# A threshold attention followed by a routed attention: the threshold as a parametric ReLU on ScalarE, transposed weights copied by VectorE, and the last queries of two pairs in 64x64 quarters of TensorE

## The chip, the cores and the metric

One core of one Trainium2 chip runs the whole program. The metric is device time in microseconds (us); lower is better. The kernel before took 880.97 us, the median of three runs (880.44 to 881.66). A run is told from no change here when it differs by more than about 0.2%, some 1.8 us.

## The reference, cut to what matters

Two attentions stand behind each other. The first has 8 batches of 8 heads, 576 queries and keys, 64 features. Every score that lies more than `tau` below the largest of its row is dropped before the softmax:

```python
scores = scale * np.matmul(q, k.transpose(0, 1, 3, 2))
thresh = np.max(scores, axis=-1, keepdims=True) - tau
scores = np.where(scores >= thresh, scores, -1000000000.0)
scores = scores - np.max(scores, axis=-1, keepdims=True)
attn = np.exp(scores)
attn = attn / (np.sum(attn, axis=-1, keepdims=True) + 1e-09)
return np.matmul(attn, v).astype(np.float32)
```

The heads are put side by side (512 features), and the second attention, called MoE below, projects them for four experts of 64 features, does a causal softmax attention for each, multiplies by an output matrix and adds the two experts that a gate picks for each row. The change does not touch its arithmetic.

## The kernel before, in words

Work goes by **pairs** of heads: 32 pairs (8 batches of 4), and the two heads of a pair lie in partitions 0 to 63 and 64 to 127. After the four pairs of a batch comes the MoE part of that batch (`moe`).

For pair n, `prep` loads k, q and v, transposes k and q on TensorE and lets ScalarE copy them to `kx` and `qx`. The 576 queries are cut into four **main tiles** of 128 (s = 0 to 3) and a **tail** of 64 (s = R = 4).

- `scores` (line 821). A main tile makes two score blocks of 128 queries by 576 keys, one for each head, in four matmuls of 64 rows by 128 columns of the array, so that both heads use one half each. The tail makes one block: head 0's 64 queries in partitions 0 to 63, head 1's in 64 to 127, by four matmuls on 128 rows and 64 columns, with the zero padded tiles `tk` and `tq`. For each block of 128x576, VectorE copies PSUM to `sc` and takes the row minimum (`copied_min`, line 661; q is scaled by -1/8, so it is minus the maximum), GpSimd adds tau to it (`thr`, line 628, one column), ScalarE takes `exp` (line 672), VectorE compares with `thr`, multiplies and sums the row (`stt`, line 650), VectorE inverts the sum (lines 627 and 639), and GpSimd multiplies the row by it (line 628) into `pp`.
- `transp` and `transp_tails` transpose `pp` in 128x64 pieces on TensorE (line 1161), and `blocks_out` lets ScalarE copy the two PSUM banks into `pt`, `pt4` and `ptt` (line 600).
- `attnv` multiplies by v (64 columns of the array for each head) and splits the result into a high and a low part `x`.

Nothing is run in the order in which the code names it. A `Plan` records every operation with a key, which is its pair's number plus an offset from the table `PLACE` (by step) and one from `PLACE_OP` (by engine and tile). `arrange` plays them on five engines with fixed costs and writes down the order, and each engine then runs its own list strictly in that order. Where the planner foresees TensorE idle in the first 80 us, `fill` puts in matmuls on a constant tile `still` (line 1158), whose result nobody reads. Buffers come from small families (`SLOTS`: 5 of `pp`, 3 of `sc`, 5 of `pt`). All eight PSUM banks are shared: scores take two neighbouring banks a block (family `s`), all else one (family `g`).

Of the kernel before, what the change touches and what calls it, by code (L numbers as in the profile page):

```python
# [22 lines left out]
SLOTS = {"ki": 2, "qi": 2, "qx": 2, "kx": 2, "pp": 5, "st": 2, "vm": 2, "p2": 3, "sc": 3, "pt": 5, "pt4": 2,  # L23
         "ptt": 2, "x": 12, "v2": 1, "q2": 2, "zt": 2, "z0": 2, "z1": 2, "pt2": 4}
PLACE = {
# [19 lines left out]
    "av1": 1.4444, "kT": -1.0327, "later": 1.7433, "load": -1.3911, "perm": 3.2453, "qT": -0.7341, "qload": -1.2168,  # L45
# [4 lines left out]
}  # L50
PLACE_OP = {
    "ACT gw": 0.1842, "ACT kx": -0.5027, "ACT lg": 1.2177, "ACT p2": 1.9457, "ACT pp": -1.6841, "ACT pt": -2.7791,
    "ACT pt2": 1.5279, "ACT pt4": 0.1304, "ACT ptt": -3.9332, "ACT q2": -3.6685, "ACT q2d0": -2.4746,
    "ACT q2d1": -1.3511, "ACT qi": -2.1752, "ACT qx": 1.2312, "ACT tau_t": 1.1034, "ACT tq0": -1.9086,
    "ACT v2": 4.4888, "ACT warm": 1.5459, "ACT wkh": 2.3421, "ACT woh": -1.794, "ACT wqh": -1.3238, "ACT wvh": 3.8984,
    "ACT x": -4.5167, "ACT z0": 3.8315, "ACT z1": 1.547, "ACT zt": 2.9762, "DVE col": 0.2892, "DVE gate": -3.09,
    "DVE gt": 1.9765, "DVE gw": 5.359, "DVE lg": 1.016, "DVE p2": 3.9028, "DVE pp": -0.5531, "DVE q2": 6.2857,
    "DVE qsc": -2.8622, "DVE sc": -0.1035, "DVE st": -1.4447, "DVE still": -0.4814, "DVE tau_p": 0.8807,
    "DVE v2": 2.0003, "DVE warm": 0.2939, "DVE x": 0.3195, "DVE z0": 2.2304, "DVE z1": 0.159, "DVE zt": 2.0055,
    "PE g": -1.5017, "PE s": 1.4698, "POOL col": -3.0293, "POOL ident": 6.5183, "POOL mask": 2.2701,  # L60
    "POOL mask2": -1.5054, "POOL p2": -1.7322, "POOL pp": 1.1515, "POOL q2d0": 1.9326, "POOL q2d1": -0.4273,
    "POOL st": -4.7961, "POOL tie": -4.1632, "POOL tk0": -1.7488, "POOL tk1": -4.6506, "POOL tq0": 3.2991,
    "POOL tq1": -0.284, "POOL vtx0": 0.099, "POOL vtx1": -1.8361, "POOL vtz0": -1.5424, "POOL vtz1": -1.4797,
    "POOL wkl": 0.1504, "POOL wol": 2.3037, "POOL wql": 1.3512, "POOL wvh": -0.2325, "POOL wvl": -5.4675,
    "SP ki": 0.3554, "SP lg": 0.4166, "SP out": -1.7257, "SP qi": 1.0657, "SP st": 0.188, "SP tk0": 2.4441,
    "SP tk1": -6.0235, "SP tq0": 1.1743, "SP tq1": -1.2151, "SP vm": -1.3425, "SP vtx0": -1.0912, "SP vtx1": 1.4099,
    "SP vtz0": -1.3099, "SP vtz1": 1.2953,
}
AV_GROUPS = ((4, 0, 1), (2, 3))
AHEAD = 3  # L70
LAST_OUT = 3
CHANGE = ((0, 150, 205, 150), (205, 0, 205, 150), (205, 150, 0, 0), (205, 150, 60, 0))
EXP_SB = True
# [55 lines left out]
class Op:  # L129
    def __init__(self, e, busy, late, outs, ins, fn, at):  # L130
        self.e, self.busy, self.late, self.outs, self.ins, self.fn = e, busy, late, outs, ins, fn
        self.base, self.unit = at
        own = f"{self.unit}@{self.base:g}"
        self.unit = own if own in PLACE else self.unit
        self.kind = e + " " + (outs[0].v.fams[0] if outs else "out")
        self.key = self.base + PLACE[self.unit]
        self.mode = 0
        self.pre = set()
        self.dma = False
# [6 lines left out]
class Plan:  # L146
# [68 lines left out]
    def network(self):  # L215
# [43 lines left out]
        for v in tiles:  # L259
            if inside(v):  # L260
                g = of[v.ops[0]]
                needs[g].append(v)
                for n in v.ops:
                    if ops[n].e != "PE":
                        for r in ops[n].outs:
                            if r.v not in needs[g] and not any(ops[x].e == "PE" for x in self.writers(r.v)):
                                needs[g].append(r.v)
# [14 lines left out]
    def arrange(self):  # L282
# [11 lines left out]
        for v in sorted(tiles, key=lambda v: (turn[v], v.index)):  # L294
            if not inside(v) and v.fams[0] != "col":
# [14 lines left out]
        tiled = [0]  # L310

# [22 lines left out]
        def allot(g, t):  # L334
            got, taken, step = [], set(), defaultdict(int)
            for v in needs[g]:
                if v.slot is not None:
                    continue
                if not inside(v) and v.fams[0] != "col":
# [15 lines left out]
        while wake:  # L355
# [19 lines left out]
            for v, s in got:  # L375
# [3 lines left out]
                if not inside(v) and v.fams[0] != "col":  # L379
# [8 lines left out]
            if ops[g].dma:  # L388
                t = max(t, landed[-8])
                landed.append(t + ops[g].late)  # L390
            at[g] = t
# [95 lines left out]
def kernel(  # L487
# [48 lines left out]
    def const(name, shape, dtype=F32):  # L536
# [5 lines left out]
             "p2": 2 * SM, "sc": S, "pt": 2 * SM, "pt4": 7 * P, "ptt": 2 * P, "x": S, "v2": (R + 1) * E * D, "q2": 2 * S,  # L542
# [15 lines left out]
    def matmul(o, x, y, start, stop):  # L558
        w = size(y)
        rows, cols = x.shape[0], size(x)  # L560
        form = 2 if rows == 64 else 1 if cols == 64 else 0
# [6 lines left out]
        if form:  # L568
            t /= 2
# [4 lines left out]
    def transposed(x, y, blocks):  # L574
        for n, (a, b) in enumerate(blocks):
            for o, i, sl in ((x, a, heads[0]), (y, b, heads[1])):
                half_transpose(o[:, n * D:(n + 1) * D], i[sl], sl)
# [97 lines left out]

    def dma(dst, src, e="SP", more=0):
# [21 lines left out]
    tau_p = const("tau_p", [P, 1])  # L698
    qsc = const("qsc", [P, 1])
# [8 lines left out]
    scaled("DVE", tau_p, tau_t, 0.0, op0=ALU.max)  # L708
# [58 lines left out]

    def values_in(n):
        b, hp = divmod(n, NPAIR)
        plan.place = (n, "vload")  # L770
        vm = plan.tile("vm", [P, 2, R, D], F32)
        dma(vm, v[b, 2 * hp:2 * hp + 2, :SM, :].rearrange("h (p r) d -> p h r d", r=R))
        for j in range(2):
            dma(vtz[n % 2][heads[j], j], v[b, 2 * hp + j, SM:, :])
            dma(vtx[n % 2][heads[1 - j], j], v[b, 2 * hp + j, SM:, :])
        return vm, vtz[n % 2], vtx[n % 2]

    def prep(n):
# [3 lines left out]
        tk, tq = tks[n % 2], tqs[n % 2]  # L782
# [4 lines left out]
        plan.place = (n if n else -30.0, "load")  # L787
        for j in range(2):
            dma(ki[:, :, j], ks[:, :, j], "SP", more)
        plan.place = (n if n else -29.0, "qload" if n else "load")  # L790
        for j in range(2):
            dma(qi[:, :, j], qs[:, :, j], eq, more)
        plan.place = (n if n else -22.0, "tload" if n else "load")
        for j in range(2):
            dma(tk[heads[j], heads[j]], k[b, 2 * hp + j, SM:, :], "SP", more)
        for j in range(2):
# [395 lines left out]
```

## Time and profile before

| what | value |
|---|---|
| runs | 880.97 us median (880.44 to 881.66) |
| the profiled execution's own time | 884.14 us |
| its span on the core, first to last instruction | 882.4 us |
| mean granted TensorE clock | 0.996 |
| TensorE busy | 846.4 us (96%) |
| VectorE busy | 692.8 us (79%) |
| ScalarE busy | 660.2 us (75%) |
| GpSimd busy | 425.5 us (48%) |

Busy is the union of an engine's instructions. A matmul's modelled end lies well behind the start of the next one, so a busy TensorE can still be waiting a little. An engine's idle time is put down to the event that ended it. Lines are those of the kernel before; the helpers record one line for all their callers, so an operation is told by line and tile together.

### The profile page before, as it was taken

What the parts mean: (1) busy time and instruction counts of PE and PEld (TensorE: products, weight loads), DVE (VectorE), ACT (ScalarE), POOL (GpSimd) and SP (SyncE); (2) the same over time, 40 slices, a digit from 0 to 9 for tenths busy, and PEclk for the clock granted to TensorE, in tenths of its full rate; (3) what the DMA queues carried; (4) which work ended last, traced back from release to release, by engine and by line L of the source; (5) the groups of instructions that cost most, each with busy time, mean ns of one, the idle gap of its engine ahead of it and who ended that gap; (6) DMA issues with size and microseconds to landing.
All of it is one profiled execution on the core that took longest, in us unless ns stands there. A gap on an engine that the chain in (4) does not pass through costs nothing.

```text
span 882.4 us, 29749 instructions
## 1 busy us (share of the span) xinstructions
PE 846.4 (96%) x11579; PEld 715.3 (81%) x11579; DVE 692.8 (79%) x2309; ACT 660.2 (75%) x1560; POOL 425.5 (48%) x757
## 2 busy tenths in 40 slices
PE   9799999999999999999999999999999999999998
PEld 6676887879887798878887888877888779887896
DVE  5888777887868868788778877798886987869475
ACT  5768777987778767787687867788777976778564
POOL 6767444654446435364344643555434643447201
PEclk9999999999999999999999999999999999999999
DMA  5532110121111211212111221121211221100002
GB/s 116 121 72 57 43 44 20 46 64 32 51 42 45 75 36 39 56 45 55 42 43 44 54 55 44 40 56 50 49 53 33 49 54 35 39 16 15 14 13 85
DMA packets 109645, 42.83 MB, mean 49 GB/s; under 512 B 96320, under 2 KB 104768, under 8 KB 109504
## 3 DMA queue, kind: packets, MB, share of 16 engines
q1 hardware_dynamic: 108144, 40.64, 18.0%
q8 instruction: 91, 1.49, 0.7%
q10 hardware_dynamic: 1360, 0.30, 0.2%
q14 instruction: 50, 0.41, 0.2%
HBM read 31.47 MB, written 9.44 MB: 46 GB/s over the span
## 4 chain that ended last, share of the span: by engine, by line
PE 60%; DVE 20%; POOL 9%; ACT 5%; issue 5%; DMA 1%; POOLq 0%; DVEq 0%; ACTq 0%
PE banks L571 49%; PE banks L1161 10%; DVE pp L650 5%; DVE sc L661 5%; POOL pp L628 3%; POOL p L628 3%; DVE p L656 2%; ACT pp L672 2%; POOL col L628 2%; ACT pt L600 2%; DVE col L627 2%; DVE x L611 1%; DVE gate L611 1%; DVE col L639 1%; PE banks L1158 1%
## 5 line engine op out<-in xcount | busy, mean ns | idle before, releaser
L628 POOL TENSOR_SCALAR pp<-pp,col 128x576 f32<-128x576 f32 x284 | 213.1, 758 | 238.6 <-DVE col L639 189.1
L650 DVE SCALAR_TENSOR_TENSOR pp<-sc,col,pp 128x576 f32<-128x576 f32 x284 | 239.8, 867 | 45.8 <-ACT pp L672 24.9
L600 ACT ACTIVATE pt<-banks 128x512 f32<-128x512 f32 (+3 forms) x448 | 225.7, 568 | 45.2 <-PE banks L1161 43.3
L661 DVE TENSOR_SCALAR_CACHE_REDUCE sc<-banks 128x576 f32<-128x576 f32 x288 | 207.6, 750 | 58.6 <-PE banks L571 56.4
L672 ACT ACTIVATE pp<-sc,col 128x576 f32<-128x576 f32 x284 | 209.8, 776 | 57.1 <-DVE sc L661 52.9
L571 PE MATMUL banks<-kx,qx 64*128 64x288 f32 (+1 forms) x1280 | 199.4, 425 | 3.0 <-DVE sc L661 2.0
L571 PE MATMUL banks<-pt,vm 128*64 128x128 f32 (+1 forms) x2560 | 154.1, 264 | 0.8 <-DVE sc L661 0.7
L628 POOL TENSOR_SCALAR col<-col,tau_p 128x1 f32<-128x1 f32 x288 | 91.4, 321 | 116.9 <-DVE sc L661 84.2
L571 PEld LDWEIGHTS banks<-pt,vm 128*64 128x64 f32 x2560 | 132.6, 137 | 15.7 <-issue 5.0
L571 PEld LDWEIGHTS banks<-kx,qx 64*128 64x128 f32 (+1 forms) x1280 | 108.9, 179 | 36.4 <-issue 4.9
L1161 PEld LDWEIGHTS banks<-ident,pp 64*128 64x128 f32 x2624 | 99.5, 139 | 40.8 <-POOL pp L628 15.2
L1161 PE MATMUL banks<-ident,pp 64*128 64x64 f32 x2624 | 117.5, 227 | 14.8 <-POOL pp L628 11.6
L628 POOL TENSOR_SCALAR p<-p,col,gw 128x384 f32<-128x384 f32 (+3 forms) x116 | 85.5, 743 | 78.4 <-DVE col L639 32.8
L672 ACT ACTIVATE p<-p,col 128x256 f32<-128x256 f32 (+4 forms) x138 | 79.4, 584 | 7.3 <-DVE col L656 7.2
L656 DVE CUSTOM_DVE_ANT_0 p<-banks,mask 128x256 f32<-128x256 f32 (+4 forms) x138 | 67.3, 510 | 10.0 <-PE banks L571 9.9
L571 PE MATMUL banks<-wvh,x 128*128 128x260 f32 x320 | 63.5, 288 | 0.0
L571 PE MATMUL banks<-x,wqh 128*128 128x288 f32 x256 | 54.1, 303 | 0.0
L571 PEld LDWEIGHTS banks<-wvh,x 128*128 128x128 f32 x320 | 51.1, 188 | 1.6 <-issue 0.2
L571 PE MATMUL banks<-x,wkh 128*128 128x288 f32 x256 | 51.9, 295 | 0.0
L571 PE MATMUL banks<-pt,v 128*64 128x128 f32 (+1 forms) x960 | 50.8, 258 | 0.0
L627 DVE TENSOR_SCALAR col<-col 128x2 f32<-128x2 f32 (+1 forms) x240 | 47.0, 199 | 3.7 <-ACT pp L672 0.2
L600 ACT ACTIVATE x<-banks 128x256 fp32r<-128x256 f32 (+1 forms) x96 | 28.2, 331 | 28.3 <-PE banks L571 28.0
(120 smaller groups left out, 1318.8 us busy)
## 6 DMA issues: line engine op xcount, KB each, us to landing
ki<-in_k_dram SPq DMA_DIRECT2D x64, 128.0 KB, 2.8
vm<-in_v_dram SPq DMA_DIRECT2D x32, 256.0 KB, 2.8
qi<-in_q_dram SPq DMA_DIRECT2D x62, 128.0 KB, 2.6
out_dram<-st SPq DMA_DIRECT2D x28, 256.0 KB, 2.0
out_dram<-st SPq DMA_DIRECT2D x10, 128.0 KB, 2.3
tk<-in_k_dram SPq DMA_DIRECT2D x64, 16.0 KB, 2.3
vtz<-in_v_dram SPq DMA_DIRECT2D x64, 16.0 KB, 2.4
vtx<-in_v_dram SPq DMA_DIRECT2D x64, 16.0 KB, 2.2
```

The lines of the kernel that those rows point to most:

```text
L571: lambda o, x, y: nc.tensor.matmul(o, x, y, start=start, stop=stop))
L600: run(e, t, [dst], [src], lambda d, s: nc.scalar.activation(d, s, AF.Copy))
L611: lambda d, a, b: (nc.vector if e == "DVE" else nc.gpsimd).tensor_tensor(d, a, b, op=op))
L627: return m.tensor_scalar(d, s, x_, None, op0=op0)
L628: return m.tensor_scalar(d, s, x_, y_, op0=op0, op1=op1)
L639: run("DVE", 80, [x], [x], lambda d, s: nc.vector.reciprocal(d, s))
L650: return nc.vector.scalar_tensor_tensor(d, a_, x_, r.pop(0), op0=op0, op1=op1, **kw)
L656: lambda o, a, i, m: nc.vector.tensor_tensor_reduce(o, i, m, 1.0, 3e38, ALU.add, ALU.min, a))
L661: lambda o, a, i: nc.vector.tensor_scalar(o, i, 1.0, None, op0=ALU.mult, op1=ALU.min, accum_out=a))
L672: return nc.scalar.activation(d, s, AF.Exp, scale=scale, **kw)
L1158: nc.tensor.matmul(banks[:, n, :256], still_[:, :P], still_[:, :1].to_broadcast([P, 256]), start=True, stop=True)
L1161: o.fn(*(r.place() for r in (*o.outs, *o.ins)))
```

## The change

There are four parts, and a new order.

1. **Threshold and sum.** `stt` goes. ScalarE runs a parametric ReLU instead (`kinked`): its input is `thr` minus `sc`, that is, how far a score lies above the threshold; what is positive stays, what is negative is multiplied by 1e36. A second ScalarE pass takes `exp` of it minus tau and gives the row sum at once. GpSimd's `thr` is made for both heads in one instruction of 128x2, after both minima.
2. **Copies.** The PSUM copies of the transposed weights `pt` go from ScalarE to VectorE; those of the short tails `ptt` stay on ScalarE.
3. **Tails of two pairs.** An even pair has no tail tile any more. In the odd pair behind it the tails of both pairs become one tile of two blocks (one for each head, pair in partitions 0 to 63 and 64 to 127), by eight matmuls on 64 rows and 64 columns. From there on it is treated as a main tile; `transp_tails`, `pt4`, `vtx` and the padding are gone. `qx`, `kx`, `v` of the even pair are kept until then.
4. **Buffers and planner.** `sc` has 4 buffers (and is not handed out in a fixed sequence any more), `pt` 6. The planner knows a shared port of VectorE and GpSimd and a cost for changes to and from quarters. `PLACE` and `PLACE_OP` have new numbers and separate names for odd pairs.

```diff
-SLOTS = {"ki": 2, "qi": 2, "qx": 2, "kx": 2, "pp": 5, "st": 2, "vm": 2, "p2": 3, "sc": 3, "pt": 5, "pt4": 2,
+SLOTS = {"ki": 2, "qi": 2, "qx": 2, "kx": 2, "pp": 5, "st": 2, "vm": 2, "p2": 3, "sc": 4, "pt": 6, "tk": 2, "tq": 2,
...
-    "t21": 1.0599, "t30": 1.4234, "t31": 1.3617, "t40": 0.4129, "t41": 1.1318, "tT": -0.5068, "tload": -2.0284,
+    "t30": 1.2303756, "tload": 1.6494662, "tt0": 0.8962797, "tt1": 1.2616384, "vload": 8.0012586, "w0": 0.8425372,
...
-AV_GROUPS = ((4, 0, 1), (2, 3))
+AV_GROUPS = (((0, 1), (2, 3)), ((4, 0, 1), (2, 3)))
...
+    def kinked(dst, src, x):
+        run("ACT", cost("ACT", size(src), inps(src)) + 100, [dst], [src, x],
+            lambda d, s, x: nc.scalar.activation(d, s, AF.Prelu, bias=x, scale=-1.0, alpha=1e36))
...
         for hf in range(2):
             for j, rows in enumerate(heads):
                 o = hf * HS + (ST if j == 0 else 0)
-                if s < R:
-                    matmul(sp[j][:, hf, :HS], qx[rows, s * P:(s + 1) * P], kx[rows, o:o + HS], True, True)
-                else:
-                    matmul(sp[0][rows, hf, :HS], qx[:, SM + j * ST:SM + (j + 1) * ST], kx[:, o:o + HS], True, True)
+                for i, (qx, kx) in enumerate(qks):
+                    if s < R:
+                        matmul(sp[j][:, hf, :HS], qx[rows, s * P:(s + 1) * P], kx[rows, o:o + HS], True, True)
+                    else:
+                        matmul(sp[j][heads[i], hf, :HS], qx[rows, SM:SM + ST], kx[rows, o:o + HS], True, True)
+        cs = []
         for j in range(nj):
...
-            copied_min(c, sv, nmx[:, js])
-            scaled("POOL", thr[:, js], nmx[:, js], 1.0, tau_p, ALU.mult, ALU.add)
+            copied_min(cs[j], sp[j][:, :, :HS], nmx[:, j:j + 1])
+        scaled("POOL", thr, nmx, 1.0, tau_p, ALU.mult, ALU.add)
+        for j, c in enumerate(cs):
+            unit(n, f"s{s}{j}")
             e = halves(pp[:, j * S:(j + 1) * S])
-            exp(e, c if EXP_SB else sv, bias=nmx[:, js], scale=-1.0)
-            stt(e, c, thr[:, js], e, ALU.is_le, ALU.mult, accum=ss[:, js])
+            kinked(e, c, thr[:, j:j + 1])
+            exp(e, e, bias=tau_n, accum=ss[:, j:j + 1])
         inverse(ss[:, :nj])
...
-        return blocks_out([(pp[:, o:o + P],) * 2 for o in cols], plan.tile("pt", [P, 2 * SM], F32))
+        return blocks_out([(pp[:, o:o + P],) * 2 for o in cols], plan.tile("pt", [P, 2 * SM], F32), "DVE")
...
-        order = (4, 0, 1, 2, 3)
+        held[n % 2] = (qx, kx), vm, vt
+        odd = n % 2
+        order = (R, 0, 1, 2, 3) if odd else (0, 1, 2, 3)
+        pp, pt = {}, {}
         for s in order:
-            pp[s] = scores(n, s, qk)
+            pp[s] = scores(n, s, [held[i][0] for i in range(2)] if s == R else [(qx, kx)])
```

What this does to the lists of the engines is shown at three places. First **TensorE (PE) at a tail tile**. In the order before it stands between transposes of two other tiles and the products with v of its own pair; 64x288 is one tail matmul's result, 128x288 a main tile's:

```order
L1161 MATMUL banks_161<-ident_163,pp3_72 128x64 x16
L1161 MATMUL banks_161<-ident_163,p21_79 128x64 x16
L571 MATMUL banks_161<-kx1_68,qx1_66 64x288 x4
L571 MATMUL banks_161<-pt40_89,vm0_76 64x64 x8
L571 MATMUL banks_161<-pt40_89,vtx0_181 64x64 x2
L571 MATMUL banks_161<-pt4_88,vm0_76 64x128 x8
```

Now one such place serves two pairs, with `kx0` and `qx0` of the even pair and `kx1` and `qx1` of the odd one in turn:

```order
L587 MATMUL banks_165<-kx1_68,qx1_66 128x288 x4
L587 MATMUL banks_165<-kx0_67,qx0_65 64x288
L587 MATMUL banks_165<-kx1_68,qx1_66 64x288
L587 MATMUL banks_165<-kx0_67,qx0_65 64x288
L587 MATMUL banks_165<-kx1_68,qx1_66 64x288
L587 MATMUL banks_165<-kx0_67,qx0_65 64x288
L587 MATMUL banks_165<-kx1_68,qx1_66 64x288
L587 MATMUL banks_165<-kx0_67,qx0_65 64x288
L587 MATMUL banks_165<-kx1_68,qx1_66 64x288
L587 MATMUL banks_165<-pt0_85,vm0_76 64x128 x8
```

The 32 places with four tail matmuls each have become 16 with eight each, and the products with v behind them are those of a main tile. Second, **ScalarE (ACT) in the middle of the program**, where attention of one batch and MoE of the one before are mixed. Before, each block has one `exp` (line 672), and the copies of line 600 stand between them:

```order
L672 ACTIVATE pp0_69<-sc2_83,col17_135 128x576
L672 ACTIVATE pp0_69<-sc0_81,col17_135 128x576
L600 ACTIVATE pt41_90<-banks_161 128x7x64 x2
L600 ACTIVATE pt0_84<-banks_161 128x8x64 x2
L672 ACTIVATE pp4_73<-sc1_82,col16_134 128x576
L672 ACTIVATE pp4_73<-sc2_83,col16_134 128x576
L600 ACTIVATE x2_95<-banks_161 128x256
```

Now line 699 is the parametric ReLU and line 693 the `exp` with the row sum:

```order
L699 ACTIVATE pp2_71<-sc0_81,col14_136 128x576
L699 ACTIVATE pp2_71<-sc2_83,col14_136 128x576
L693 ACTIVATE pp2_71,col10_132<-pp2_71,tau_n_173 128x576 x2
L693 ACTIVATE p20_78,col20_142<-p20_78,col2_124 128x384
L699 ACTIVATE pp3_72<-sc3_84,col17_139 128x576
L699 ACTIVATE pp3_72<-sc1_82,col17_139 128x576
L693 ACTIVATE pp3_72,col19_141<-pp3_72,tau_n_173 128x576
L621 ACTIVATE x0_97<-banks_165 128x256
```

The 320 copies of `pt` and `pt4` of the attention are gone from this list, and 288 passes of the parametric ReLU have come into it. Third, **VectorE (DVE)** at about the same place. Before, two blocks go through `copied_min` (line 661) and `stt` (line 650):

```order
L661 TENSOR_SCALAR sc1_82,col23_141<-banks_161 128x576
L661 TENSOR_SCALAR sc2_83,col23_141<-banks_161 128x576
L602 COPY st1_75<-banks_161 128x512
L650 SCALAR_TENSOR_TENSOR pp2_71,col25_143<-sc1_82,col24_142,pp2_71 128x576
L650 SCALAR_TENSOR_TENSOR pp2_71,col25_143<-sc2_83,col24_142,pp2_71 128x576
```

Now copies of transposed weights (line 623) stand where `stt` stood:

```order
L682 TENSOR_SCALAR sc0_81,col27_149<-banks_165 128x576
L648 TENSOR_SCALAR col18_140<-col18_140 128x2
L682 TENSOR_SCALAR sc2_83,col27_149<-banks_165 128x576
L660 RECIPROCAL col18_140<-col18_140 128x2
L623 COPY pt1_86<-banks_165 128x8x64 x2
```

So 288 instructions on SBUF have left this engine's list and 288 that read PSUM have come in.

## Rows read from the trace of the kernel before

**Rows 1.** The page, part 1: busy time, share of the span, instructions.

```profile
PE 846.4 (96%) x11579; PEld 715.3 (81%) x11579; DVE 692.8 (79%) x2309; ACT 660.2 (75%) x1560; POOL 425.5 (48%) x757
```

**Rows 2.** Busy us by stretch: PE, PEld, DVE, ACT, POOL; clock, DMA share, GB/s.

```profile
500.00:540.00 40.00, 40.00 (x539) 33.93 (x537) 30.80 (x94) 29.21 (x63) 16.35 (x32) 1.00 0.21 52
580.00:620.00 40.00, 37.80 (x626) 31.36 (x622) 35.70 (x117) 34.21 (x81) 24.11 (x42) 1.00 0.19 49
100.00:820.00 720.00, 700.03 (x9733) 595.44 (x9733) 583.55 (x1963) 556.92 (x1322) 351.08 (x616) 1.00 0.17 44
```

**Rows 3.** The page, part 4: shares of the chain that ended last.

```profile
PE 60%; DVE 20%; POOL 9%; ACT 5%; issue 5%; DMA 1%; POOLq 0%; DVEq 0%; ACTq 0%
PE banks L571 49%; PE banks L1161 10%; DVE pp L650 5%; DVE sc L661 5%; POOL pp L628 3%; POOL p L628 3%; DVE p L656 2%; ACT pp L672 2%; POOL col L628 2%; ACT pt L600 2%; DVE col L627 2%; DVE x L611 1%; DVE gate L611 1%; DVE col L639 1%; PE banks L1158 1%
```

**Rows 4.** Timeline of PE, 318 to 325 us: start, us, what, count.

```profile
319.47 1.19 PE L571 MATMUL banks<-kx,qx 128*64 128x288 f32 x8
320.49 0.63 PE L571 MATMUL banks<-pt,vm 128*64 128x64 f32 x16
...
323.35 0.71 PE L1161 MATMUL banks<-ident,pp 64*128 64x64 f32 x16
323.90 1.19 PE L571 MATMUL banks<-kx,qx 64*128 64x288 f32 x8
324.93 0.28 PE L1161 MATMUL banks<-ident,qi 64*128 64x64 f32 x4
```

**Rows 5.** Timeline of PE, first tail tile, windows ending at 8.72, 9.05, 9.14, 9.30.

```profile
8.71 0.46 PE L571 MATMUL banks<-kx,qx 128*64 128x288 f32 x1
8.71 0.70 PE L571 MATMUL banks<-kx,qx 128*64 128x288 f32 x2
8.71 0.88 PE L571 MATMUL banks<-kx,qx 128*64 128x288 f32 x3
8.71 0.94 PE L571 MATMUL banks<-kx,qx 128*64 128x288 f32 x4
```

**Rows 6.** Groups by line and form: count, busy us, mean ns, idle before.

```profile
L650 DVE SCALAR_TENSOR_TENSOR pp<-sc,col,pp 128x576 f32<-128x576 f32 x284 | 239.8, 867 | 45.8 <-ACT pp L672 24.9 <-POOL col L628 19.5 <-ACT ptt L600 0.3
L672 ACT ACTIVATE pp<-sc,col 128x576 f32<-128x576 f32 x284 | 209.8, 776 | 57.1 <-DVE sc L661 52.9 <-DVE col L639 1.2 <-POOL pp L628 0.9
L600 ACT ACTIVATE pt<-banks 128x512 f32<-128x512 f32 x288 | 155.9, 604 | 25.9 <-PE banks L1161 24.3
L628 POOL TENSOR_SCALAR col<-col,tau_p 128x1 f32<-128x1 f32 x288 | 91.4, 321 | 116.9 <-DVE sc L661 84.2 <-DVE col L627 21.9 <-DVE col L639 10.2
L600 ACT ACTIVATE pt<-banks 128x448 f32<-128x448 f32 x64 | 32.4, 541 | 13.2 <-PE banks L1161 13.1
L672 ACT ACTIVATION_READ_ACCUMULATOR p<-p,col 128x1 f32 x138 | 27.5, 199 | 0.0
L602 DVE COPY st<-banks 128x512 f32<-128x512 f32 x32 | 22.1, 689 | 8.5 <-PE banks L571 8.5
L600 ACT ACTIVATE ptt<-banks 128x128 f32<-128x128 f32 x64 | 14.2, 279 | 0.4 <-PE banks L1161 0.4
L598 ACT ACTIVATE qx<-banks,qsc 128x320 f32<-128x320 f32 x64 | 31.4, 529 | 3.4 <-PE banks L1161 2.4
L600 ACT ACTIVATE kx<-banks 128x320 f32<-128x320 f32 x64 | 25.3, 434 | 1.6 <-PE banks L1161 1.5
```

**Rows 7.** Timeline of ACT, 341 to 348 us.

```profile
341.52 1.46 ACT L672 ACTIVATE pp<-sc,col 128x576 f32<-128x576 f32 x2
...
347.02 0.72 ACT L672 ACTIVATE p<-p,col 128x512 f32<-128x512 f32 x1
347.63 0.20 ACT L672 ACTIVATION_READ_ACCUMULATOR p<-p,col 128x1 f32 x1
347.73 0.72 ACT L672 ACTIVATE p<-p,col 128x512 f32<-128x512 f32 x1
```

**Rows 8.** Busy time of the instructions with tile pp, 580 to 620 us.

```profile
580.00:620.00 40.00, 7.34 (x164) 6.08 (x164) 15.02 (x33) 13.46 (x18) 11.51 (x15) 1.00 0.19 49
```

More of the change, by code (lines that the diff above doesn't have):

```diff
@@ L265, in network @@
                         for r in ops[n].outs:
-                            if r.v not in needs[g] and not any(ops[x].e == "PE" for x in self.writers(r.v)):
+                            if r.v not in needs[g] and r.v.fams[0] != "sc" and not any(ops[x].e == "PE" for x in self.writers(r.v)):
                                 needs[g].append(r.v)
@@ L338, in allot @@
                     continue
-                if not inside(v) and v.fams[0] != "col":
+                if not inside(v) and v.fams[0] not in ("col", "sc"):
                     f = v.fams[0]
@@ L378, in arrange @@
                     held[u] = v
-                if not inside(v) and v.fams[0] != "col":
+                if not inside(v) and v.fams[0] not in ("col", "sc"):
                     head[v.fams[0]] += 1
@@ L390, in arrange @@
                 landed.append(t + ops[g].late)
+            if ops[g].port == 1:
+                t = max(t, port[1])
+                port[0] = t + busy[g] - 50
+            elif ops[g].port:
+                t = max(t, port[0])
+                if ops[g].port == 2:
+                    port[1] = t + busy[g] - 200
             at[g] = t
@@ L568, in matmul @@
         if form:
-            t /= 2
+            t /= 4 if form == 4 else 2
         plan.op("PE", t, t + more + 20, [o], [x, y],
@@ L786, in prep @@
         more = 0 if n > 1 else 100
-        plan.place = (n if n else -30.0, "load")
+        unit(n, "load")
+        if not n:
+            plan.place = (-30.0, "load")
         for j in range(2):
             dma(ki[:, :, j], ks[:, :, j], "SP", more)
-        plan.place = (n if n else -29.0, "qload" if n else "load")
+        unit(n, "qload")
+        if not n:
+            plan.place = (-29.0, "load")
         for j in range(2):
             dma(qi[:, :, j], qs[:, :, j], eq, more)
[L793 to L796, printed above, removed]
-            dma(tq[heads[j], heads[j]], q[b, 2 * hp + j, SM:, :], eq, more)
+        unit(n, "tload")
+        if not n:
+            plan.place = (-22.0, "load")
+        for rows in heads:
+            dma(tk[rows], k[b, hs, SM:, :].rearrange("h p d -> p h d"), "SP", more)
+        dma(tq[heads[0]], q[b, hs, SM:, :].rearrange("h p d -> p h d"), eq, more)
         kx, qx = plan.tile("kx", [P, SM + 3 * ST], F32), plan.tile("qx", [P, SM + P], F32)
         for name, x, tail, o in (("kT", ki, tk, kx), ("qT", qi, tq, qx)):
-            plan.place = (n, name)
+            unit(n, name)
             gs = [gbank() for _ in range(2)]
@@ L850, in scores, with blocks_out @@
         return pp
-    def blocks_out(blocks, out):
+    def blocks_out(blocks, out, e="ACT"):
         gs = [gbank() for _ in range(2)]
@@ L862, in transp @@
     def transp(n, s, pp):
-        plan.place = (n, f"t{s}0")
+        unit(n, f"t{s}0")
         cols = [j * (S + ST) + c * P for j in range(2) for c in range(R)]
-        return blocks_out([(pp[:, o:o + P],) * 2 for o in cols], plan.tile("pt", [P, 2 * SM], F32))
-    def transp_tails(tiles, pp):
-        main = [s for s in tiles if s < R]
-        blocks = [(pp[s][:, SM:SM + P],) * 2 for s in main]
-        if R in tiles:
-            p = pp[R]
-            blocks = [(p[:, c * P:(c + 1) * P], p[:, ST + c * P:ST + (c + 1) * P]) for c in range(R)] + blocks
-            blocks.append((p[:, S - P:S], p[:, :P]))
-        return blocks_out(blocks, plan.tile("pt4" if R in tiles else "ptt", [P, len(blocks) * P], F32))
@@ new lines, in attnv @@
+            at = ptt[:, tiles.index(s) * P:(tiles.index(s) + 1) * P]
+            for i, (vm, vt, xs) in enumerate(pairs if s == R else pairs[-1:]):
+                m, sub = (P, slice(0, P)) if s < R else (ST, heads[i])
+                gs = g[:, o:o + m]
+                for c in range(R):
+                    for j in range(2):
+                        x = pt[s][:, (j * R + c) * P:(j * R + c + 1) * P][:, sub]
+                        matmul(gs[heads[j]], vm[:, j, c], x, c == 0, False)
+                for j in range(2):
+                    matmul(gs[heads[j]], vt[:, j], at[:, sub], False, True)
+                if s < R and parts and parts[-1][3] == s * P:
+                    parts[-1][1:4:2] = o + m, s * P + m
+                else:
+                    parts.append([o, o + m, s * P, s * P + m, xs])
+                o += m
@@ L917, in pair @@
                         XT[b, hp] = [plan.tile("x", [P, S], F32R) for _ in range(2)]
-                    plan.place = (n, f"tt{k_}")
-                    ptt = transp_tails(tiles, pp)
-                    plan.place = (n, f"av{k_}")
-                    attnv(tiles, qk, pt, ptt, XT[b, hp])
+                    unit(n, f"tt{k_}")
+                    ptt = blocks_out([(pp[x][:, SM:SM + P],) * 2 for x in tiles], plan.tile("ptt", [P, len(tiles) * P], F32))
+                    unit(n, f"av{k_}")
+                    attnv(tiles, [(*held[i][1:], XT[b, hp - odd + i]) for i in range(odd + 1)], pt, ptt)
     def projected(b, ep, base, pre, parts):
```

140 lines of the change are left out of this document (63 added, 77 removed), and 51 rows, old and new, of the table PLACE.

## The prediction

> **What bounds the kernel now.** I began with the busy time of the engines. TensorE is at 96%, VectorE at 79%, ScalarE at 75%, GpSimd at 48% [rows 1]; the granted clock is 0.996 over the span, so the clock leaves nothing to gain. Then I cut the span into stretches, because these shares are averages over two kinds of work. Between 100 and 820 us TensorE is idle for 720 - 700.0 = 20.0 us in all [rows 2]. Where MoE products prevail (500 to 540 us) it is never idle and VectorE has 30.8 of 40 us. Where attention prevails (580 to 620 us) it is idle for 2.2 us while VectorE has 35.7 and ScalarE 34.2 of 40 [rows 2]. Such a stretch comes about once a batch, so some eight times. Last I read the chain that ended last: 60% TensorE, 20% VectorE, 9% GpSimd, 5% ScalarE, and `stt` alone has 5%, 44 us [rows 3]. So TensorE sets the end for most of the time, and in attention-heavy stretches VectorE and ScalarE are close behind or ahead. A shorter TensorE list should show in the time nearly in full; a VectorE relief only in those stretches; a ScalarE load costs nothing until ScalarE fills there.
>
> **TensorE.** A tail tile takes 1.02 us from its first matmul to the first one behind it (319.47 to 320.49), as long as a main tile with the same number of instructions (323.90 to 324.93) [rows 4]. Eight instructions, two for each matmul, run on two parts of the array at once, so one instruction holds its part for 1.02 / 4 = 0.25 us. Before, two pairs need two tail tiles, 2.04 us. Now they need one with 16 instructions on four quarters. If four run at once it is 16 / 4 x 0.25 = 1.02 us, a gain of 1.02 us; if only two run at once it is 2.04 us and nothing is gained. These are the two ends, as the trace shows no quarter. I take four at once because of the first tail tile. There the second matmul waits for its own operand, so that its half starts late: by 9.05 us two instructions have started, the third between 9.05 and 9.14 (the second matmul's first), the fourth before 9.30 [rows 5]. The fourth cannot be the second matmul's other instruction, whose part is taken for 0.25 us; it is the third matmul's, on the half that was free. Parts of the array thus go on without waiting for each other. 16 places x 1.02 = 16.3 us.
>
> The Trainium skill (TensorE: Matmul & The Clock Gate, Part 3: Packing small matmuls) says the opposite of what this needs: matmuls start and end strictly in program order. With two instructions of one matmul behind each other on the same quarter, that would put only two quarters to work, and the gain of 16.3 us would be none; the start in [rows 5] that overtakes an earlier instruction speaks against the rule here.
>
> Entering a new form costs something, but the lists have as many changes between whole, half-column, half-row and quarter forms as before (about 350 in each), so I cost it at nothing; by either end it is below 0.1 us at 16 places. The order has 64 transposes fewer. Sixteen take 0.55 us (323.35 to 323.90) [rows 4], 0.034 us each, so 2.2 us at most; 32 of them lose only one of two that ran side by side, so I take 1.5.
>
> **VectorE.** 288 `stt` go, 239.8 us of busy time [rows 6]. 288 copies of 128x512 from PSUM come; the same form of `st` takes 0.689 us [rows 6], so 198 us. Sixteen small sums and reciprocals go. The engine falls from 692.8 to about 650 us. No instruction of this list was long enough alone to hold the end, so this is worth something only through waits.
>
> **ScalarE.** It gains 288 passes of the parametric ReLU, which no row shows. The nearest is `exp` on the same 576 columns with one column operand, 0.776 us, 209.8 / 284 = 0.739 us of busy time [rows 6]. An operand more is bounded by `qx` against `kx`, 0.529 to 0.434 for equal columns [rows 6], 0.1 us above; the lower bound is the bare distance of two such instructions, 1.46 - 0.776 = 0.68 [rows 7]. I take 0.739: +212.8. Each `exp` now reads its sum out. The read takes 0.199 us [rows 6] as one bound, but with it a 512-column `exp` starts again after 0.71 us (347.02 to 347.73) [rows 7], and 0.68 for 576 without it makes about 0.63 for 512: 0.08 is the other. I take 0.09: +26. Of the 288 copies of 128x512, 256 are the attention's and go, at 155.9 / 288 = 0.541 us: -138.6; 64 of 128x448 go: -32.4; 32 more short tails at 0.222 and 32 longer ones come: +16 [rows 6]. The sum is 660.2 + 212.8 + 26 - 138.6 - 32.4 + 16 = 744 us, or 86% of a span of 865.
>
> In the stretch from 580 to 620 us ScalarE runs 18 blocks [rows 8]. Each adds 0.739 + 0.09 and sheds (138.6 + 32.4 - 16) / 288 = 0.54, so 0.29 net: 34.2 + 5.2 = 39.4 of 40 us. VectorE falls by 15.0 [rows 8] and rises by 18 x 0.689 = 12.4, to 33.1. So the fullest engine beside TensorE goes from 35.7 us (VectorE) to 39.4 (ScalarE) there. What hides ScalarE's extra work is the MoE work beside it: from 100 to 820 us ScalarE has 556.9 of 720 us [rows 2], and 82% of 288 x 0.29 = 84 us added gives 626, or 87%, which is less than the 89% that VectorE holds in its fullest stretch. If the new order spreads attention more evenly, it is hidden; if not, see the fourth case. Behind a waiting parametric ReLU stand the copies of q, k, `ptt` and x on ScalarE's list, and TensorE waits for those; but the copies of `pt`, which free PSUM banks, no longer stand there, which helps. I charge 2 us for it.
>
> **GpSimd** loses 144 of 288 instructions for `thr`, 144 x 0.32 = 46 us [rows 6]; it is at 48%, so I count nothing. Its wait is new in one respect: `thr` of head 0 must now wait for head 1's minimum, one VectorE pass, before ScalarE may begin; five `pp` and four `sc` buffers are the cover, and without it it is part of the fourth case. Loads are fewer (95 issues off the queue of SP) and hidden.
>
> **The sum.** The profiled execution took 884.1 us, 3.2 above the median of the runs. 884.1 - 16.3 - 1.5 + 2 = 868.3, less 3.2: 865 us.
>
> **The rivals.**
> First, the forecast: quarters four at once, ScalarE hidden. 865 us, own range 858 to 873. For it: TensorE at 97% of the steady stretch.
> Second, VectorE's relief also counts. `stt` has 44 us of the chain [rows 3], and VectorE's 35.7 in the attention-heavy stretch becomes 33. If half of TensorE's 20 us of steady idle time goes with it, and the 2 us charged are not due, it is 865 - 12 = 853 us. Against it: what VectorE drops from the chain, ScalarE takes up, with two passes one behind the other in place of one on each engine.
> Third, quarters run two at a time. Then 16 tiles of 2.04 us stand against 32 of 1.02, and 865 + 16 = 881 us: no change. Against it: [rows 5]; for it: no quarter has been seen.
> Fourth, on the other side: ScalarE becomes the bound in the attention-heavy stretches. If an engine in strict order can be kept no busier there than VectorE was, 35.7 / 40 = 89%, then 39.4 us of ScalarE work need 44.1: 4.1 us more, eight times, 33 us. Against the gain of 17.8 it is 884.1 - 17.8 + 33 = 899, less 3.2: 896 us at the full price. It decides as soon as the loss is over 17.8 / 8 = 2.2 us a stretch, that is, if ScalarE cannot be kept above 39.4 / 42.2 = 93%. With partial spreading 883 to 896; I put it at 890. Against it: the averages above leave room to spread.
> The Trainium skill (ScalarE: Activation LUTs, Rules for kernel authors) says to put relu, max and multiply on VectorE and not on ScalarE. By that rule the threshold moves the wrong way, which is this fourth case; its reason, VectorE's speed with short types and one source, is not met in [rows 6], where the fused fp32 pass takes 0.867 us on VectorE and a like pass 0.776 on ScalarE.
>
> **How the numbers follow.** Forecast 0.50, second 0.20, third 0.10, fourth 0.20. Faster by more than 0.2% (about 1.8 us, what a measurement tells from no change) is the first two: 0.70. The third is the same, 0.10. The fourth is slower, 0.20. The likeliest case alone gives 858 to 873; for 8 in 10 the range takes in the second case down to 849, the third, and the fourth up to 889, which leaves out its upper half.
>
> **What would show it.** In the new profile the eight tail matmuls should take about 1.0 us to the first instruction behind them; 2.0 would be the third case. TensorE's busy time should fall by some 18 us. The parametric ReLU should have about 0.78 us, ScalarE about 744 us of busy time and VectorE about 650. In the waits, `exp` and the parametric ReLU should not have become what transposes of `pp` wait for; if TensorE's idle time before transposes and products with v has grown by more than 18 us and ScalarE stands over 95% in stretches of 40 us, the fourth case holds. The prediction is wrong if the new order loses at other places what the tails gain, for instance at the start, where TensorE waits for the weights' preparation.

## The result, and the profile after

The changed kernel takes 858.56 us (median of four runs, 856.88 to 859.20) against 880.75 of the kernel before on the same chip: a ratio of 0.974, 95% interval 0.973 to 0.976, 22.2 us less. The forecast was 865 us, faster, with a range from 849 to 889. The way and the range are right; the gain is 22 us where 16 were worked out, and the experiments show that the sum came out close by errors of both signs, so that its nearness is in part luck.

The profiled execution took 858.49 us, its span is 856.8. The busy line of its page, to be read against [rows 1]:

```profile
PE 827.5 (97%) x11478; PEld 705.9 (82%) x11478; DVE 621.1 (72%) x1990; ACT 712.3 (83%) x1880; POOL 350.6 (41%) x607
```

TensorE has 18.9 us less, where some 18 were forecast, and its idle time fell from 882.4 - 846.4 = 36.0 to 29.3 us. (The execution of the kernel before that was profiled took 884.14 us, 3.4 above the median, so some 3 us of the difference between the two pages are not the change's.) VectorE lost 71.7 us and ScalarE gained 52.1: they have changed places. The same stretches as in [rows 2], and one where ScalarE is fullest (columns as there):

```profile
500.00:540.00 40.00, 40.00 (x450) 34.68 (x449) 28.88 (x92) 30.91 (x81) 14.08 (x23) 1.00 0.18 50
580.00:620.00 40.00, 39.10 (x550) 33.52 (x548) 28.67 (x89) 33.88 (x88) 16.85 (x30) 1.00 0.22 55
100.00:820.00 720.00, 703.95 (x9924) 604.70 (x9922) 531.92 (x1706) 607.36 (x1612) 292.71 (x497) 1.00 0.17 44
140.00:180.00 40.00, 38.16 (x630) 31.38 (x624) 31.59 (x105) 38.13 (x101) 20.05 (x35) 1.00 0.17 41
```

Where attention prevails (140 to 180 us) ScalarE is now at 95%, and TensorE idles for 1.8 us, about as it did beside VectorE at 89% before (2.2 us). Of the twenty stretches of 40 us from 20 to 820 us, nine now hold ScalarE at 90 to 95%; before, none held it above 86%. The passes of the parametric ReLU alone (line 699: ScalarE's busy us and count) in two of them:

```profile
140.00:180.00 40.00, 12.19 (x18) 1.00 0.17 41
460.00:500.00 40.00, 13.13 (x19) 1.00 0.19 49
```

So the densest stretches hold 18 and 19 blocks of attention, as many as the 18 of [rows 8]. At the start, in the first 100 us, TensorE idles for 9.9 us; before it was 11.6.

The chain that ended last, against [rows 3]:

```profile
PE 69%; ACT 18%; DVE 6%; POOL 3%; issue 3%; SPq 0%; DMA 0%; POOLq 0%; DVEq 0%; ACTq 0%
PE banks L587 58%; PE banks L1183 10%; ACT pp L699 7%; ACT pp L693 7%; DVE sc L682 2%; DVE pt L623 2%; POOL pp L649 2%; PE banks L1180 1%; POOL p L649 1%; ACT p L693 1%; ACT pt L621 1%; ACT x L621 1%; DVE col L648 1%; ACT ptt L621 1%; POOL col L649 1%
```

The 20% of VectorE and 5% of ScalarE have become 6% and 18%; the two passes (lines 699 and 693) stand where `stt` and the minima stood. Neither holds up a transpose directly: before transposes of `pp` TensorE waits 2.1 us for GpSimd's rows, where it waited 11.6.

A tail of two pairs on TensorE's timeline. The first two rows come from windows that end 0.03 and 0.35 us after its start, the last two from the whole:

```profile
205.55 0.47 PE L587 MATMUL banks<-kx,qx 64*64 64x288 f32 x4
205.55 0.72 PE L587 MATMUL banks<-kx,qx 64*64 64x288 f32 x8
205.55 1.20 PE L587 MATMUL banks<-kx,qx 64*64 64x288 f32 x16
206.68 1.09 PE L587 MATMUL banks<-pt,vm 128*64 128x128 f32 x16
```

Four instructions start within 0.03 us, the next four before 0.35 us: four quarters work at once. The 16 take 206.68 - 205.55 = 1.13 us, 0.11 more than the tail of [rows 4], which has as many steps on each part of the array. There the products with v behind the tail have the tail's own form; here a new form follows. Nine of the 32 tails of the kernel before were followed by another form too, and they took 404.15 - 403.03 = 1.12 us, as here:

```profile
403.03 1.19 PE L571 MATMUL banks<-kx,qx 128*64 128x288 f32 x8
404.15 0.71 PE L1161 MATMUL banks<-ident,pp 64*128 64x64 f32 x16
```

Added up over the whole trace, from the first matmul of each tail to the first one behind it, the 32 tails of before hold 34.8 us and the 16 of now 19.0: 15.8 us less.

The groups that answer to [rows 6], and ScalarE's list in a full stretch (start, us, what):

```profile
L693 ACT ACTIVATE pp<-pp,tau_n 128x576 f32<-128x576 f32 x288 | 222.5, 778 | 0.2
L699 ACT ACTIVATE pp<-sc,col 128x576 f32<-128x576 f32 x288 | 211.1, 776 | 24.5 <-POOL col L649 23.2
L623 DVE COPY pt<-banks 128x512 f32<-128x512 f32 x288 | 182.8, 682 | 8.8 <-PE banks L1183 8.3
L693 ACT ACTIVATION_READ_ACCUMULATOR pp<-pp,tau_n 128x1 f32 x288 | 58.3, 202 | 0.0
```

```profile
159.68 0.79 ACT L699 ACTIVATE pp<-sc,col 128x576 f32<-128x576 f32 x1
160.35 0.79 ACT L693 ACTIVATE pp<-pp,tau_n 128x576 f32<-128x576 f32 x1
161.02 0.21 ACT L693 ACTIVATION_READ_ACCUMULATOR pp<-pp,tau_n 128x1 f32 x1
161.11 0.79 ACT L693 ACTIVATE pp<-pp,tau_n 128x576 f32<-128x576 f32 x1
161.78 0.21 ACT L693 ACTIVATION_READ_ACCUMULATOR pp<-pp,tau_n 128x1 f32 x1
161.89 1.44 ACT L699 ACTIVATE pp<-sc,col 128x576 f32<-128x576 f32 x2
```

The parametric ReLU takes 0.776 us, the same as `exp` did. Behind one another each pass starts 0.67 us after the one before (159.68, 160.35), and an `exp` with its sum 0.76 to 0.78 (160.35, 161.11, 161.89).

### The profile page after: what moved, and what is told of

It is laid out like the page before. It is cut to its first block, busy times and chain, and to the rows that moved or that the text cites. A ratio compares the mean times of both kernels' runs of the same rounds, so it can differ in the third digit from the quotient of the medians.

```text
span 856.8 us, 28908 instructions
## 1 busy us (share of the span) xinstructions
PE 827.5 (97%) x11478; PEld 705.9 (82%) x11478; DVE 621.1 (72%) x1990; ACT 712.3 (83%) x1880; POOL 350.6 (41%) x607
## 4 chain that ended last, share of the span: by engine, by line
PE 69%; ACT 18%; DVE 6%; POOL 3%; issue 3%; SPq 0%; DMA 0%; POOLq 0%; DVEq 0%; ACTq 0%
PE banks L587 58%; PE banks L1183 10%; ACT pp L699 7%; ACT pp L693 7%; DVE sc L682 2%; DVE pt L623 2%; POOL pp L649 2%; PE banks L1180 1%; POOL p L649 1%; ACT p L693 1%; ACT pt L621 1%; ACT x L621 1%; DVE col L648 1%; ACT ptt L621 1%; POOL col L649 1%
## 5 line engine op out<-in xcount | busy, mean ns | idle before, releaser
L699 ACT ACTIVATE pp<-sc,col 128x576 f32<-128x576 f32 x288 | 211.1, 776 | 24.5 <-POOL col L649 23.2
L682 DVE TENSOR_SCALAR_CACHE_REDUCE sc<-banks 128x576 f32<-128x576 f32 x288 | 208.0, 751 | 21.0 <-PE banks L587 18.8
L693 ACT ACTIVATE pp<-pp,tau_n 128x576 f32<-128x576 f32 x288 | 222.5, 778 | 0.2
L623 DVE COPY pt<-banks 128x512 f32<-128x512 f32 x288 | 182.8, 682 | 8.8 <-PE banks L1183 8.3
L649 POOL TENSOR_SCALAR col<-col,tau_p 128x2 f32<-128x2 f32 x144 | 38.9, 270 | 232.1 <-DVE sc L682 154.1
L693 ACT ACTIVATE p<-p,col 128x512 f32<-128x512 f32 (+2 forms) x138 | 82.1, 604 | 18.3 <-DVE col L677 18.2
L649 POOL TENSOR_SCALAR p<-p,col,gw 128x512 f32<-128x512 f32 (+3 forms) x117 | 71.2, 619 | 44.3 <-DVE gw L632 30.2
L677 DVE CUSTOM_DVE_ANT_0 p<-banks,mask 128x512 f32<-128x512 f32 (+2 forms) x138 | 68.2, 514 | 21.4 <-PE banks L587 17.1
L632 DVE TENSOR_TENSOR x<-banks,x 128x256 fp32r<-128x256 f32 (+1 forms) x96 | 31.1, 351 | 58.1 <-ACT x L621 57.9
L621 ACT ACTIVATE pt<-banks 128x384 f32<-128x384 f32 (+2 forms) x128 | 57.5, 512 | 7.6 <-PE banks L1183 6.3
L587 PE MATMUL banks<-ptt,vtz 128*64 128x128 f32 (+1 forms) x640 | 58.9, 263 | 0.0
L693 ACT ACTIVATION_READ_ACCUMULATOR pp<-pp,tau_n 128x1 f32 x288 | 58.3, 202 | 0.0
```

What stands on the lines that cost most here:

```text
L587: lambda o, x, y: nc.tensor.matmul(o, x, y, start=start, stop=stop))
L621: run(e, t, [dst], [src], lambda d, s: nc.scalar.activation(d, s, AF.Copy))
L623: run(e, t, [dst], [src], lambda d, s: nc.vector.tensor_copy(d, s))
L632: lambda d, a, b: (nc.vector if e == "DVE" else nc.gpsimd).tensor_tensor(d, a, b, op=op))
L649: return m.tensor_scalar(d, s, x_, y_, op0=op0, op1=op1)
L677: lambda o, a, i, m: nc.vector.tensor_tensor_reduce(o, i, m, 1.0, 3e38, ALU.add, ALU.min, a))
```

## The experiments

In e1 and e3 to e7 a load is added to a kernel whose order stays as it was; e2 reorders eight matmuls. The loads give a price: how much of a microsecond added on an engine shows in the time. It is a price for adding. No run took work away with the order kept, and that may give back less.

**e1: the tail's matmuls twice, changed kernel.**

```diff
-                lambda o, x, y: nc.tensor.matmul(o, x, y, start=start, stop=stop))
+                lambda o, x, y: [nc.tensor.matmul(o, x, y, start=start, stop=stop) for _ in range(2 if form == 4 else 1)])
```

> The changed kernel, each of the eight matmuls of a tail of two pairs issued twice in place (the second repeats the first); the order of all else is the same. Theory: TensorE sets the end, so a tail tile grows from 0.97 to about 1.94 us and the run by 16 x 0.97 = 15.5 us, to about 874. Rival (the gain came from VectorE's relief and the new order, TensorE's saving being hidden): under 5 us more, below 864.

868.43 us, 9.9 more than the changed kernel (ratio to the kernel before 0.986, 0.984 to 0.987). A tail on its timeline:

```profile
106.65 2.23 PE L587 MATMUL banks<-kx,qx 64*64 64x288 f32 x32
108.81 1.09 PE L587 MATMUL banks<-pt,vm 128*64 128x128 f32 x16
```

2.16 us, 1.03 more at 16 places, 16.5 us; 60% of it shows. That is about halfway between the 15.5 us of the theory and the 5 us of the rival: TensorE sets the end for part of the time.

**e2: the tail quarter by quarter, changed kernel.** The loop over the halves of the keys goes innermost:

```diff
-        for hf in range(2):
-            for j, rows in enumerate(heads):
...
+            for j, rows in enumerate(heads):
+                for i, (qx, kx) in enumerate(qks):
+                    for hf in range(2):
```

> The changed kernel, the tail's eight matmuls issued quarter by quarter (both halves of the keys of one quarter behind each other) instead of going round the four quarters. Theory (each quarter goes on by itself): four instructions of one quarter stand before the first of the next, and the tile still takes about 1.0 us, the run stays within 2 us of 858.6. Rival (matmuls start strictly in program order): only neighbours overlap; thirteen steps of 0.24 us, 3.1 us a tile, 16 x 2.1 = 34 us more, about 893.

857.01 us (0.973, 0.971 to 0.974), not told from the changed kernel.

```profile
206.29 1.22 PE L587 MATMUL banks<-kx,qx 64*64 64x288 f32 x16
207.44 0.77 PE L587 MATMUL banks<-pt,vm 128*64 128x128 f32 x10
```

1.15 us a tile although four instructions of one quarter stand in a row: the quarters go on independently, and the rival falls.

**e3: 128x128 copies behind the parametric ReLU, changed kernel.**

```diff
+                             nc.scalar.activation(spare, s[:, 0, :P], AF.Copy)))
```

> The changed kernel with one copy of 128x128 added on ScalarE behind each of the 288 parametric ReLUs; the order of all else is the same. Some 0.2 us each, 58 us more on ScalarE, 83% to 90% busy. Theory (ScalarE's added work is hidden beside MoE work): under a fifth shows, less than 12 us more, below 871. Rival (ScalarE sets the end where attention prevails, and has given part of the gain back): over half shows, 29 us more, 888 or above.

891.73 us (1.012, 1.010 to 1.014), 33.2 more. Its page, parts 1 and 4:

```profile
PE 846.0 (95%) x11478; PEld 712.3 (80%) x11478; DVE 625.3 (70%) x1990; ACT 766.7 (86%) x2168; POOL 350.3 (39%) x607
...
PE 50%; ACT 32%; DVE 9%; issue 4%; POOL 3%; DMA 1%; SPq 0%; ACTq 0%; POOLq 0%; DVEq 0%
```

54.4 us more on ScalarE cost 33.2: 61% shows, and ScalarE's share of the chain goes from 18% to 32%. The theory falls: ScalarE's load is not hidden, though the engine is busy for only 83%.

Where it is lost can be read from the two traces, since TensorE's instructions come in the same order in both. Counted along that order, the profiled execution falls behind that of the changed kernel by 35.0 us, and 22.9 of them come in the nine stretches in which ScalarE was at 90 to 95%. These hold about half of the added copies, some 28 us of load, so 0.8 of it shows there. In the rest it is 12.2 of some 26 us, a little under half.

**e4: the same load on VectorE, changed kernel.**

```diff
+                                 nc.vector.tensor_copy(spare, i[:, 0, :P])))
```

> The changed kernel with one copy of 128x128 from PSUM added on VectorE behind each of the 288 minima; order of all else the same. Some 0.2 us each, 58 us more on VectorE. Theory (TensorE sets the end, VectorE at 72% has room): less than 12 us more. Rival (VectorE's relief was a good part of the gain, so that giving 58 us of it back costs most of what was won beyond 17.8 us): 10 us or more, and more than the same load on ScalarE costs.

876.53 us (0.994, 0.993 to 0.996), 18.0 more for 675.7 - 621.1 = 54.6 us: 33%. It misses the theory, and the rival in part, since ScalarE's load costs nearly twice as much. The added copy also holds its PSUM bank for longer (TensorE and its weight loads waited for these copies 15 times, 10.1 us in all), and that is in the price.

**e5, e6, e7: the same three loads on the kernel before.** The edits are those of e3 (behind `exp`), e4 and e1.

> The kernel before with one copy of 128x128 added on ScalarE behind each of the 288 exponentials of the threshold attention (the same load of about 54 us that cost the changed kernel 33 us); order unchanged. Theory (before, VectorE stood next behind TensorE, and the change has put ScalarE in its place): ScalarE had more room, so it costs under 22 us, below 903. Rival (any 54 us on ScalarE cost the same, whichever kernel): 28 to 38 us, 909 to 919.

> The kernel before with one copy of 128x128 from PSUM added on VectorE behind each of the 288 minima (about 54 us, which cost the changed kernel 18 us); order unchanged. Theory (VectorE at 79% was a second bound before and is none now): over 28 us, above 909. Rival (VectorE's room did not matter in either): 13 to 22 us, 894 to 903.

> The kernel before with each of the four matmuls of a pair's tail issued twice in place; 32 tiles grow by about 0.97 us, 31 us on TensorE; order unchanged. Theory (TensorE sets the end, but part of it is hidden behind VectorE and ScalarE, as in the changed kernel, where 60% of an added load showed): 18 to 25 us, 899 to 906. Rival (all of it shows): 29 us or more, 910 or above.

The busy lines of e5 and e6, and a doubled tail of e7:

```profile
PE 851.2 (95%) x11579; PEld 715.0 (80%) x11579; DVE 697.6 (78%) x2309; ACT 710.2 (80%) x1848; POOL 427.5 (48%) x757
```

```profile
PE 850.5 (96%) x11579; PEld 718.8 (81%) x11579; DVE 739.2 (83%) x2597; ACT 668.7 (75%) x1560; POOL 427.4 (48%) x757
```

```profile
110.75 2.21 PE L571 MATMUL banks<-kx,qx 128*64 128x288 f32 x16
112.74 0.69 PE L571 MATMUL banks<-pt,vm 128*64 128x64 f32 x16
```

| load | changed kernel | kernel before |
|---|---|---|
| TensorE | e1: 9.9 of 16.5 us, 0.60 | e7: 908.39 us (1.029, 1.027 to 1.031), 26.1 of 32 x 0.97 = 31, 0.84 |
| ScalarE | e3: 33.2 of 54.4, 0.61 | e5: 892.73 (1.011, 1.009 to 1.013), 10.5 of 50.0, 0.21 |
| VectorE | e4: 18.0 of 54.6, 0.33 | e6: 891.45 (1.010, 1.008 to 1.013), 9.2 of 46.4, 0.20 |

For the kernel before, TensorE set the end for most of the time. The theory of e5 holds. That of e6 falls: VectorE at 79% was no second bound, and its load cost less than the rival's 13 us, too. After the change ScalarE is a second bound. e7 came a little over the theory's 25.

**e8: the quarters, without the new threshold and copies.** Threshold and copies are as in the kernel before; planner and buffers stay those of the changed kernel, and the tables of offsets are searched anew:

```diff
-            kinked(e, c, thr[:, j:j + 1])
-            exp(e, e, bias=tau_n, accum=ss[:, j:j + 1])
+            exp(e, c, bias=nmx[:, j:j + 1], scale=-1.0)
+            stt(e, c, thr[:, j:j + 1], e, ALU.is_le, ALU.mult, accum=ss[:, j:j + 1])
...
-        return blocks_out([(pp[:, o:o + P],) * 2 for o in cols], plan.tile("pt", [P, 2 * SM], F32), "DVE")
+        return blocks_out([(pp[:, o:o + P],) * 2 for o in cols], plan.tile("pt", [P, 2 * SM], F32))
```

> The changed kernel with the threshold by a VectorE pass and the copies of the weights on ScalarE as before; the tails of two pairs in quarters stay. The order is planned anew, with its tables of offsets searched anew by the planner's own costs. Theory (the quarters are the larger part: 17.8 us of TensorE, of which 60 to 78% show): 867 to 872. Rival A (the quarters are all of it): 857 to 862. Rival B (the threshold and the copies are most of it): 874 or above.

865.91 us (0.980, 0.978 to 0.983), 16.5 less than the kernel before and just under the theory's 867. It is not the quarters alone that brought it, as e10 shows: the new planner is in it.

**e9: threshold and copies alone,** put into the kernel before, which keeps its 3 `sc` and 5 `pt`. The order is searched anew, by a planner that may choose the buffer of `sc` but does not know the shared port.

> The kernel before with the threshold as a parametric ReLU, the row sum and the copies of the weights as in the changed one; each pair keeps its own tail in half columns. Order planned and searched anew. Theory (load moved from VectorE to ScalarE, neither of which sets the end alone: small): 872 to 884. Rival (most of the gain): 868 or below.

880.56 us (0.998, 0.997 to 0.999): 1.8 us less, at the limit of what can be told and within the theory. ScalarE has 735.1 us (84%) in it and 24% of the chain:

```profile
PE 57%; ACT 24%; DVE 10%; POOL 4%; issue 2%; DMA 1%; SPq 0%; POOLq 0%; ACTq 0%; DVEq 0%
```

**e10: the planner alone.** Every operation and the number of buffers as before; the planner gets the shared port and the free choice of `sc`, and its tables are searched anew:

```diff
...
+            if ops[g].port == 1:
+                t = max(t, port[1])
+                port[0] = t + busy[g] - 50
...
```

> The kernel before, with the planner's shared port and its free choice of the buffer for sc, and its order searched anew; no operation changes. Theory (the order is not what brought the gain): 878 to 890. Rival (a better order is worth the rest of the 22 us by itself): 876 or below.

868.39 us (0.983, 0.980 to 0.986), 14.0 less with no operation changed. The theory falls. The order lets TensorE run through: its idle time falls from 36.0 to 866.7 - 841.5 = 25.2 us and it has 78% of the chain, with VectorE (80%) and ScalarE (76%) as busy as before:

```profile
PE 78%; DVE 11%; issue 3%; ACT 3%; POOL 3%; DMA 1%; ACTq 0%; DVEq 0%; POOLq 0%
```

This changes what the other runs are to be compared with. Beside e10 the changed kernel is 8 to 10 us faster (by the ratios 0.974 and 0.983, and by the times), and e8 only 2.5 us. That is what new operations brought on top of a new planner, as far as single searches can tell.

**e11: e8 with its search carried on.** Only the tables differ:

```diff
-    "LMo0": 4.4700925, "LMo1": 6.3049119, "LMo2": 8.4349189, "LMo3": 9.0858294, "LMo4": 4.0, "La00": 6.2268594,
+    "LMo0": 5.195294, "LMo1": 7.6870973, "LMo2": 9.1655346, "LMo3": 7.6659576, "LMo4": 4.0, "La00": 7.7105205,
```

> As e8 (quarters, old threshold and copies), with the search for its order carried on from e8's for about as long again. Theory (the threshold and the copies are worth little once the order fits the operations): 858 to 864, at most 5 us above the changed kernel. Rival (they are worth 7 us or more, as e8 against the changed kernel would say): it stays at 864 or above.

873.62 us (0.991, 0.990 to 0.993), 7.7 us more than e8: the order of a longer search, by the planner's own costs, is slower on the chip. The theory falls; the rival's 864 or above came, but an order that is worse by so much says nothing of the threshold and the copies. TensorE's steady stretch, first of e8, then of e11:

```profile
100.00:820.00 720.00, 701.23 (x9865) 599.72 (x9864) 580.23 (x1940) 557.99 (x1363) 381.97 (x619) 1.00 0.17 44
```

```profile
100.00:820.00 720.00, 695.55 (x9831) 595.36 (x9830) 589.23 (x1939) 558.54 (x1361) 398.07 (x620) 1.00 0.17 43
```

The same instructions leave TensorE idle for 18.8 us in one order and 24.5 in the other. So e8 to e11 say what an order can do, but a part's worth read from two such searches is uncertain by some 8 us, which is as much as the changed kernel has on e10.

**e12: one of the two copies of k to VectorE,** on the changed kernel, order searched anew.

```diff
-                copy("ACT", d, g[:, :m * D].rearrange("p (r c) -> p r c", c=D), None if x is ki else qsc)
+                copy("DVE" if x is ki and i_ else "ACT", d, g[:, :m * D].rearrange("p (r c) -> p r c", c=D), None if x is ki else qsc)
```

> The changed kernel with one of the two copies of transposed k of each pair moved from ScalarE to VectorE (32 of 128x320, about 14 us of ScalarE's 712), order searched anew. Theory (ScalarE's load costs the changed kernel 0.61 us for each us and VectorE's 0.33): 14 x 0.28 = 4 us less, 853 to 857. Rival (the order found for it is no better than the changed kernel's, and decides): 858 to 863.

857.48 us (0.973, 0.971 to 0.974): not told from the changed kernel. ScalarE's busy time fell by only 6.2 us, to 706.1, and VectorE's rose by 14.3, to 635.4. By the prices of e3 and e4 that is 6.2 x 0.61 = 3.8 us off and 14.3 x 0.33 = 4.7 on, so nothing was to be gained; the 14 us of the theory were not there. Which of the two theories holds stays open. In e12's chain ScalarE has 6%, where the changed kernel, as fast, has 18%: the shares of a chain are no prices. No version was found that is clearly faster than the changed kernel.

## Why the prediction was right, and where it was wrong

- *Four quarters at once.* Right, by the timeline and by e2; the third rival falls. The size was nearly right, too: 15.8 us of TensorE, not 16.3. The form behind a tail, counted at nothing and at below 0.1 us, costs 0.11 us; but some of the old tails had paid it as well, which the 2.04 us for two of them left out.
- *"A shorter TensorE list should show in the time nearly in full."* This step was mis-sized. Of an added load 0.84 shows in the kernel before (e7) and 0.60 in the changed one (e1). With the transposes' 1.5 us, 17.3 us give 10 to 15 at these prices, not 17.8.
- *The order.* This is where the sum went wrong the other way. The 22.2 us need 8 to 12 more than TensorE's saving gives, and I had charged 2 us for the new order. e10 shows that a new order alone takes 14.0 us off the old operations, so an order can bring what is missing. That it did so here is argued and not shown: the changed kernel's order belongs to its operations, orders of the same operations lie up to 8 us apart (e8, e11), and the buffers that were added, one of `sc` and one of `pt`, were not run by themselves.
- *ScalarE's load.* Too high: 712.3 us came instead of 744. The passes stand in rows of two to four now, and then each costs its distance, 0.67 to 0.68 us, which was the lower bound, and not the 0.739 of the mean before. For two passes and 288 blocks that is 34 to 40 us less; the copies that left had been counted too high in the same way, which takes some of it back. The sum's readout cost 0.09 to 0.11, where 0.09 was taken.
- *VectorE's load.* Too high as well: 621.1 us instead of about 650. The new copies have 182.8 us instead of 198, and the reading of the row sum behind each `stt`, which went with it, was not counted.
- *"A ScalarE load costs nothing until ScalarE fills."* Wrong as it was used. At 83% a microsecond more costs 0.61 (e3), at 75% it cost 0.21 (e5). The averages hide the stretches at 90 to 95%, where 0.8 of it shows, and elsewhere it was not free either.
- *The fourth rival.* Its load came: 18 blocks in 40 us and ScalarE at 38.1 us, where 39.4 were worked out, so the new order did not spread attention, which the forecast had counted on. What failed is its premise that an engine in strict order can be kept no busier than VectorE's 89%: ScalarE stands at 95%, and TensorE idles no longer beside it than before.
- *VectorE's relief* (second rival). The time came out nearer to its 853 us than to 865, but not by its mechanism: at 0.20 us a microsecond (e6) the 71.7 us are worth 14, and the 52.1 put on ScalarE cost 11 at the price before and 32 at the price after. e9 has the two together at 1.8 us, with a planner that knows less than e10's, and the changed kernel is 7 us faster than e8, which is no more than two orders lie apart. These parts were not shown to gain anything.

## What to carry to other kernels

Busy shares do not give the price of a microsecond on an engine; a known load added in place, with the order frozen, does, and it takes one run. Before the parts of a change are credited, run the old operations in an order made by the same planner: here that alone took 14 us off, and the whole change took 22. And when work is moved from one engine to another, price it at the receiving engine after the move, where it cost three times as much as before.

## What the runs showed of the hardware

- Parts of the array go on without waiting for each other: four instructions of one quarter in a row do not hold up the other three (1.15 us a tile against 1.13 in turn, e2). In a strict order of all matmuls only the last of one quarter and the first of the next could lie beside each other, and the tile would have taken 13 steps. A step is (1.99 - 1.02) / 4 = 0.2425 us, by the doubled tail of e7, so that is 3.2 us. This is where the run differs from the rule of the Trainium skill (TensorE: Matmul & The Clock Gate, Part 3: Packing small matmuls) that the prediction weighed; the measurement decides.
- A parametric ReLU with one column operand takes as long as an exponential (0.776 us for 576 columns), and reading out a row sum, 0.202 us by its record, adds only 0.09 to 0.11 us to the distance of two passes.
- A tail that is followed by matmuls of another form (other rows and columns of the array) takes 0.10 to 0.11 us longer: 1.12 instead of 1.02 us in half columns, and 1.13 in quarters.
